# Threshold attention with a gated MLP on one core: attention products of 512 tokens in place of halves, and a new order on VectorE

## The chip, the core and the metric

The kernel runs on one core of a Trainium2 chip. Its engines work side by side, each through its own list of instructions in order: TensorE (PE; its weight loads are shown as PEld), VectorE (DVE), ScalarE (ACT), GpSimd (POOL) and SyncE (SP), which here issues DMAs. The metric is the device time of one execution in microseconds (us); lower is better. Times given as "the time" are medians over several executions; the profile comes from one execution, whose own time is given beside it.

## What is computed

Eight batches, eight heads, 576 tokens, head dimension 64. Scores that lie more than tau under their row's maximum are dropped, the rest goes through a softmax and multiplies v. The heads side by side are then the rows of a gated MLP ("MoE product" below) of 4608 tokens, 512 to 2048 to 512:

```
scores = scale * np.matmul(q, k.transpose(0, 1, 3, 2))
thresh = np.max(scores, axis=-1, keepdims=True) - tau
scores = np.where(scores >= thresh, scores, -1000000000.0)
attn = softmax(scores)
x = np.matmul(attn, v)            # heads side by side: 4608 x 512
h = x @ w_in
g = h * np.clip(h + 3.0, 0.0, 6.0) / 6.0
out = g @ w_out
```

## The kernel before, in words

**Units.** A pair is two heads of one batch, a quad is two pairs (16 quads in all). A quad is worked in nine slots: four of 128 query rows for its first pair, four for the second, and slot 8 for the last 64 rows of both. A slot holds both heads of a pair, so it is a tile of 128 rows x 2 x 576 keys. There are 16 x 9 = 144 slots, and one pass of the main loop, called a period n here, stands for each of them.

**Order.** Nothing is scheduled by a planner: the order of the program's statements is the order of each engine's list. From n = 22 on (N1 in the code) a period issues, by engine:

- DVE: the two maxima of slot n+1 (`sm_max`, line 302: it reads the scores from PSUM, writes them to SBUF and gives the row maximum), the reciprocal of slot n-1 (line 317), then what the list `waiting` holds (the scaling of a finished output tile into `osb`, line 423, or a query transpose), then the casts of the attention product (line 357, or 367 for the last rows), the rectifier of the MoE product where it is DVE's turn (line 391, odd periods), and the gate (line 404). In some odd periods a stream transpose of q or k follows (lines 241, 247).
- ACT: in even periods the rectifier (line 389); two exponentials of slot n (line 314) and two masks of slot n+1 (line 309).
- POOL: the bias of slot n+1 (line 305), the normalising of slot n-1 (line 322). SP then issues the DMA that transposes these probabilities into `pT`, the operand of the attention product, or into `pR` for slot 8; stores and loads follow.
- PE: a first MoE product (`mm1`, line 381 or 376), in odd periods an attention product if one is due (`av_main`, lines 346 and 349), in even periods two parts of the second MoE product (`mm2_part`, line 415), and at the end of odd periods the scores of slots n+3 and n+2 (line 287).

**PSUM.** The eight banks of 512 float columns are one tile `ps`. Scores of even slots lie in columns 128 to 703 and 1664 to 2239 (banks 0, 1, 3, 4). Scores of odd slots lie in 704 to 1279 and 2240 to 2815, and so take the first 256 columns of banks 2 and 5. Banks 2 and 5 are also those that `bank()` hands out in turn for attention products and transposes. First MoE products write bank 6 (`HB`; bank 7 in odd periods that follow an even one without second MoE parts), second ones bank 7 (`OB`). Hence three waits that the code implies:

- scores of slot n+3 (an even one, in an odd period n) may be written once the maxima of slot n+1 have read the same columns;
- scores of slot n+2 (odd) may be written once the attention product's cast has read banks 2 and 5, and once the maxima of slot n have;
- a first MoE product may be written once the gate of the period before has read bank 6.

**When a product is due.** The dictionary `products` says in which period which product is multiplied. Before, quads 0 and 1 take 512 tokens of a pair at once; from quad 2 on each pair is split into two products of 256 tokens, every second period. The function `multiply` issues them and, with the last ones of a batch, hands the first MoE products of that batch to the list `todo1`, of which one is taken in every period. An attention product is ten matmuls: four blocks of keys for each of two heads (line 346) and the last 64 keys (line 349); each head fills half of PE's columns, 64.

```
def av_main(pair, c0=0, w=512):
    ...
    pb = bank()[:, 0:w]
    av(pb, pair, pts[pair], slice(c0, c0 + w))
    return lambda: nc.vector.tensor_copy(out=xT[b][:, hp, c0:c0 + w], in_=pb)
```

**After the loop** the last products, the remaining MoE products and the stores follow.

Of the kernel before, what the change touches and what calls it, by code (L numbers as in the profile page):

```python
# [20 lines left out]
def kernel(  # L21
# [20 lines left out]
    N1 = 22  # L42
# [169 lines left out]
    def bank():  # L212
        nonlocal turn
        turn += 1
        return ps[:, (2, 5)[turn % 2], :]
# [96 lines left out]
    def sm_exp(sl, i):  # L312
        s = sl.s[:, i, :]
        nc.scalar.activation(out=s, in_=s, func=Act.Exp, accum_out=sl.rsum[:, i:i + 1])  # L314
# [26 lines left out]
    def av(pb, pair, pT, cols):  # L341
        b, hp = divmod(pair, NPAIR)
        vm, vr = vsb[b]
        for c in range(4):
            for a in range(2):
                nc.tensor.matmul(pb[a * 64:(a + 1) * 64, :], vm[:, 2 * hp + a, c * D:(c + 1) * D],  # L346
                                 pT[:, 5 * a + c, cols], start=(c == 0), stop=False)
        for a in range(2):
            nc.tensor.matmul(pb[a * 64:(a + 1) * 64, :], vr[:, a, hp, :], pT[:, 4, cols], start=False, stop=True)  # L349

    def av_main(pair, c0=0, w=512):
        b, hp = divmod(pair, NPAIR)
        if hp == c0 == 0:
            xT[b] = x_pool.tile([P, KI, 512], BF16, tag="xT", name="xT")
# [4 lines that stand above are left out]
    def av_rest(quad):  # L359
        b, g = divmod(quad, 2)  # L360
        pb = bank()
        for n in range(2):
            av(pb[:, n * 64:(n + 1) * 64], 2 * quad + n, ptr[quad], slice(n * 64, (n + 1) * 64))
        if b % 2 == 0 and g == 0:
            xR[b // 2] = x_pool.tile([P, KI, P], BF16, tag="xR", name="xR")
        o0 = 64 * (b % 2)
        return lambda: nc.vector.tensor_copy(out=xR[b // 2][:, 2 * g:2 * g + 2, o0:o0 + 64],
                                             in_=pb[:, 0:P].rearrange("p (a b) -> p a b", a=2))
# [17 lines left out]
    def mm1_relu(hps, on_act):  # L386
        r = r_pool.tile([P, 512], F32, tag="r", name="r")[:]
        if on_act:
            nc.scalar.activation(out=r, in_=hps, func=Act.Relu, bias=three[:])  # L389
        else:  # L390
            nc.vector.tensor_scalar(out=r, in0=hps, scalar1=3.0, scalar2=0.0, op0=Alu.add, op1=Alu.max)  # L391
        return r

    def mm1_gate(item, hps, r):
        b, ni, c0 = item
        if c0 is None:
            if ni % 8 == 0:
                odd[0] = go_pool.tile([P, 1024], BF16, name="go")
            out = odd[0][:, ni % 8 * P:ni % 8 * P + 512]
        else:  # L400
            c0 += (b % 2) * (S + 64)
            out = gbuf[:, ni:ni + 2, c0:c0 + 256]
            r, hps = (x.rearrange("p (n w) -> p n w", n=2) for x in (r, hps))
        nc.vector.scalar_tensor_tensor(out=out, in0=r, scalar=6.0, in1=hps, op0=Alu.min, op1=Alu.mult)  # L404
        if c0 is None and ni % 8 == 4:
            nc.sync.dma_start_transpose(out=gbuf[:, ni - 4:ni + 4, 512:512 + P], in_=odd[0][:])
# [87 lines left out]
    for quad in range(NQUAD):  # L494
        p0, p1 = 2 * quad, 2 * quad + 1
        if quad < NB:
            jobs = ((8, p0, 0, 512), (12, p1, 0, 512), (13, None, 0, 0))
        else:
            jobs = [(7 - quad % 2 + 2 * i, *of) for i, of in enumerate(
                ((p0, 0, 256), (p0, 256, 256), (p1, 0, 256), (p1, 256, 256), (None, 0, 0)))]  # L500
        for after, *of in jobs:
            products.setdefault(quad * NSLOT + after, []).append((quad, *of))

    def multiply(n):
        copies = []
        for of, pair, *columns in products.get(n, ()):
            copies.append(av_rest(of) if pair is None else av_main(pair, *columns))
            if of % 2 and pair is None:
                todo1.extend(moe_of(of // 2)[1])
            elif pair == 2 * of + 1 and of % 2 and columns[0] == 0:  # L510
                todo1.extend(moe_of(of // 2)[0])
        return copies

# [3 lines left out]
    waiting = []  # L517
    for n, sl in enumerate(queue):
        quad, slot = sl.quad, sl.slot
        b, g = divmod(quad, 2)  # L520
        now = n
        if slot in (0, 4):
            pts[2 * quad + slot // 4] = pt_pool.tile([P, 9, 512], BF16, tag="pT", name="pT")
        if slot == 8:
            ptr[quad] = ptr_pool.tile([P, 9, P], BF16, tag="pR", name="pR")
        for ahead in {0: (1, 2), 9: (3,), 16: (4,)}.get(n, (quad + 2,) if quad > 2 and slot == (2 if quad == 3 else 0) else ()):
            if ahead < NQUAD:
                load_quad(ahead)
        if slot == 0 and g == 1 and b + 1 < B:
            load_v(b + 1)  # L530
        for copy in last_keys:
            copy()
        last_keys = []
        if 0 < n <= N1:
            for i in range(2):
                sm_exp(prev, i)
        if n + 1 < len(queue):
            sm_max(queue[n + 1])
        even = n >= N1 and n % 2 == 0
        if n > N1:  # L540
            sm_recip(prev)
        for copy in waiting:
            copy()
        waiting = []

        if todo1:
            item, then = todo1.pop(0)
            h = mm1(item, OB if n > N1 and n % 2 and not pieces else HB)
            todo2.extend(then)
        else:  # L550
            item = None
        if n >= N1:
            for copy in multiply(n):
                copy()
        if item:
            mm1_gate(item, h, mm1_relu(h, on_act=even))
        copies = pe_transpose(queue[n - 2]) if n > 1 and queue[n - 2].on_chip else None
        if prev is not None and n < N1:
            sm_recip(prev)
        if copies:  # L560
            copies()
        pieces = 2 if n % 2 == 0 and todo2 else 0
        for _ in range(pieces):
            bb, mt, part = todo2.pop(0)
            mm2_part(bb, mt, part)
        if n <= N1:
            for i in range(2):
                sm_mask(sl, i)
        if n == N1:
            sm_recip(prev)  # L570
        if n >= N1:
            for i in range(2):
                sm_exp(sl, i)
            if n + 1 < len(queue):
                for i in range(2):
                    sm_mask(queue[n + 1], i)
        if n < N1:
            for copy in multiply(n):
                copy()
        if part == 3:  # L580
            waiting.append(lambda tile=(bb, mt): late.extend(mm2_out(*tile, on_act=False)))
            part = 0
        evict = []
        for job, of in turns.get(n, ()):
            if job == "k":
                (last_keys if even else evict).append(transpose_k(of))
            elif job == "q":
                if of // 2 not in qkT:
                    alloc_qk(of // 2)
                (waiting if even else evict).append(transpose_q(of))  # L590
            else:
                (last_keys if even else evict).append(transpose_rest(of, of_k=of > 0))
        for out_of_psum in evict:
            if out_of_psum:
                out_of_psum()
        if n == 0:
            warm_up(8)
        if n <= N1:
            scores(n + 2)
        elif n % 2:  # L600
            for m in (n + 3, n + 2):
                if m < len(queue):
                    scores(m)
        if n < 8:
            warm_up(6)
        if n > 0:
            sm_norm(prev)
        flush()
        if n == 0:
            start(loads, 2)  # L610
        elif n not in (4, 12, 15, 18, 21) and not 23 < n < 30 and (n < 37 or n % 2 == 0):
            start(loads, 1)
        if n < 4 or 15 < n < 20 or n > 33:
            start(vcasts, 1 if n < N1 or n % 2 else 0)
        else:
            start(casts, 2 if n in (5, 8, 11, 14) or 21 < n < 28 else 1)
        prev = sl
# [29 lines left out]
                count[1] += 1  # L647

    av_main(2 * last + 1, 0, 256)()
    for item in todo1:  # L650
        rest1(*item, on_act=False)
    sm_recip(prev)
# [45 lines left out]
```

## Time and profile before

| | |
|---|---|
| time, median of 5 executions | 522.43 us (521.38 to 523.4) |
| the profiled execution | 521.78 us, span of its instructions 520.0 us |
| granted TensorE clock | 1.000 |
| ACT and POOL, share of the span | 87% and 58% |
| scores on PE (line 287) | 174.0 us busy |
| first MoE products (381) and second (415) on PE | 130.8 and 123.4 us busy |
| attention products of 256 or 512 columns and of the last rows (346) | 39.1 us busy |
| maxima (302) on DVE | 205.1 us busy in 288 instructions |
| casts of 256 columns (357) on DVE | 23.5 us in 56, 420 ns each |
| casts of 512 columns (357) on DVE | 2.8 us in 4, 691 ns each |

How to read it: busy time is the union of an engine's instructions in the span. A matmul's own duration (273 ns at 256 columns) is longer than the time between two starts, since matmuls overlap; for what PE really needs, take the starts in the timeline. In timeline lines the columns are start, duration, engine, line, operation, output and inputs, shape, count, and in brackets the idle time before it with what ended it. Lines of one kind that follow each other are merged, and a few matmul records are missing from the trace (seven shown where eight are issued).

By stretches, the busy time of each engine is even from 104 us to 460 us (PE 57.5 of every 58.0 us, DVE 54.6, ACT 54.9). Before 80 us there are no MoE products; from 80 to 104 us there are hardly any second ones (PE 21.8 of 24 us, DVE 20.6, ACT 23.9); after 480 us the second MoE products of the end run on PE with little else.

### The profile page before, as it was taken

The numbers are of one execution on the slowest core, as the hardware profiler recorded it, in microseconds if no ns is written. First come the engines' busy times: TensorE is split into PE (matmuls) and PEld (weight loads), VectorE is DVE, ScalarE is ACT, GpSimd is POOL, SyncE is SP. The second block draws the span as 40 slices with busy tenths as digits, with TensorE's granted clock in tenths as the row PEclk, the third lists the DMA queues.
The fourth block names the chain that finished last, engine by engine and source line by source line (L and its number), as shares of the span: only waits on it lengthen the run. The fifth ranks groups of instructions, "written<-read, shape, count | busy, mean of one in ns | idle before, by whom it ended". The sixth has DMA issues, their size and how long they took to land.

```text
span 520.0 us, 12068 instructions
## 1 busy us (share of the span) xinstructions
PE 502.8 (97%) x4089; PEld 321.0 (62%) x4145; DVE 442.5 (85%) x1124; ACT 451.9 (87%) x980; POOL 299.3 (58%) x538
## 2 busy tenths in 40 slices
PE   8999899999999999999999999999999999999997
PEld 6765556666665666666655666666655666667463
DVE  3788888998999999999999999999999999877151
ACT  4999979999999999999999999999999999995060
POOL 1788869756676665657566756667566655551000
PEclk9999999999999999999999999999999999999999
DMA  5899899989999999999999999999999996564222
GB/s 131 129 171 169 143 147 146 195 140 177 167 169 165 158 179 165 179 172 185 171 157 166 178 177 158 174 167 173 172 166 165 168 170 113 112 117 65 83 61 61
DMA packets 314094, 78.77 MB, mean 151 GB/s; under 512 B 296624, under 2 KB 309168, under 8 KB 314032
## 3 DMA queue, kind: packets, MB, share of 16 engines
q1 hardware_dynamic: 294464, 67.90, 77.1%
q0 software_dynamic: 18368, 9.71, 15.5%
q8 instruction: 32, 0.52, 0.4%
q10 hardware_dynamic: 1200, 0.39, 0.3%
q14 instruction: 30, 0.25, 0.2%
HBM read 36.70 MB, written 9.44 MB: 89 GB/s over the span
## 4 chain that ended last, share of the span: by engine, by line
PE 77%; ACT 3%; DVE 2%; issue 2%; DMA 1%; POOL 0%; POOLq 0%; DVEq 0%
PE ps L287 24%; PE ps L415 23%; PE ps L381 19%; PE ps L346 6%; PE ps L376 2%; ACT s L309 1%; PE ps L349 1%; ACT s L314 1%; DMA pR<-pn 1%; ACT r L389 1%; DMA g<-go 1%; DVE s L302 1%; DVE g L404 1%; POOL pn L322 0%; PE ps L257 0%
## 5 line engine op out<-in xcount | busy, mean ns | idle before, releaser
L322 POOL TENSOR_SCALAR pn<-s,rinv 128x576 bf16<-128x576 f32 x288 | 210.6, 743 | 20.4 <-issue 4.4
L302 DVE TENSOR_SCALAR_CACHE_REDUCE s<-ps 128x576 f32<-128x576 f32 x288 | 205.1, 748 | 17.6 <-PE ps L287 9.0
L309 ACT ACTIVATE s<-s,bias 128x576 f32<-128x576 f32 x288 | 205.8, 763 | 6.0 <-POOL bias L305 5.7
L314 ACT ACTIVATE s<-s 128x576 f32<-128x576 f32 x288 | 192.5, 671 | 0.3
L287 PE MATMUL ps<-kT,qT 64*128 64x384 f32 (+7 forms) x1280 | 174.0, 419 | 4.7 <-DVE s L302 3.8
L287 PEld LDWEIGHTS ps<-kT,qT 64*128 64x128 f32 (+1 forms) x1280 | 103.6, 175 | 59.3 <-issue 15.8
L381 PE MATMUL ps<-xT,w_in_sb 128*128 128x256 bf16 x1024 | 130.8, 273 | 1.3 <-DVE g L404 0.7
L415 PE MATMUL ps<-w_out_sb,g 128*128 128x512 bf16 x524 | 123.4, 379 | 2.8 <-issue 0.2
L381 PEld LDWEIGHTS <-w_in_sb 128*128 128x128 bf16 x1024 | 95.5, 98 | 41.0 <-issue 22.1
L305 POOL TENSOR_SCALAR bias<-m 128x2 f32<-128x2 f32 x144 | 26.9, 187 | 152.9 <-DVE rinv L317 130.3
L404 DVE SCALAR_TENSOR_TENSOR g<-r,ps 128x512 bf16<-128x512 f32 x128 | 87.6, 687 | 9.6 <-ACT r L389 5.5
L415 PEld LDWEIGHTS <-g 128*128 128x128 bf16 x576 | 56.3, 98 | 56.6
L389 ACT ACTIVATE r<-ps,three 128x512 f32<-128x512 f32 x81 | 55.4, 687 | 29.0 <-PE ps L381 21.4
L314 ACT ACTIVATION_READ_ACCUMULATOR s<-s 128x1 f32 x288 | 54.5, 189 | 0.0
L391 DVE TENSOR_SCALAR r<-ps 128x512 f32<-128x512 f32 x63 | 42.9, 681 | 0.0
L346 PE MATMUL ps<-pT,vm 128*64 128x256 bf16 (+1 forms) x480 | 39.1, 285 | 0.0
L346 PEld LDWEIGHTS <-vm 128*64 128x64 bf16 x736 | 27.2, 110 | 17.0 <-issue 14.8
L357 DVE CAST xT<-ps 128x256 bf16<-128x256 f32 (+1 forms) x60 | 26.3, 438 | 12.8 <-PE ps L349 12.8
L423 DVE TENSOR_SCALAR osb<-ps 128x512 f32<-128x512 f32 x31 | 20.9, 673 | 13.3 <-PE ps L415 13.3
L302 DVE DVE_READ_ACCUMULATOR s<-ps 128x1 f32 x288 | 23.9, 83 | 0.0
L317 DVE RECIPROCAL rinv<-rsum 128x2 f32<-128x2 f32 x144 | 23.0, 160 | 0.6 <-ACT s L314 0.6
L143 POOL DMA_DIRECT2D vm<-in_v_dram x28 | 21.4, 766 | 0.7 <-issue 0.7
(57 smaller groups left out, 258.6 us busy)
## 6 DMA issues: line engine op xcount, KB each, us to landing
out_dram<-osb SPq DMA_DIRECT2D x31, 256.0 KB, 2.6
nq<-in_q_dram SPq DMA_DIRECT2D x96, 72.0 KB, 3.5
km<-in_k_dram SPq DMA_DIRECT2D x96, 64.0 KB, 3.3
vm<-in_v_dram POOLq DMA_DIRECT2D x24, 128.0 KB, 4.0
km<-in_k_dram SPq DMA_DIRECT2D x16, 128.0 KB, 3.6
w_in_sb<-in_moe_w_in_dram POOLq DMA_DIRECT2D x16, 128.0 KB, 3.6
w_out_sb<-in_moe_w_out_dram POOLq DMA_DIRECT2D x16, 128.0 KB, 4.3
pT<-pn SPq DMA_TRANSPOSE x117, 3.9
```

The source lines that it names most:

```text
L287: nc.tensor.matmul(ps_flat[rows, c0:c0 + w], qT_of(pair)[a * 64:(a + 1) * 64, q0:q0 + rows.stop - rows.start], kT_of(pair)[a * 64:(a + 1) ...
L302: nc.vector.tensor_scalar(out=sl.s[:, i, :], in0=ps_flat[:, c0:c0 + S], scalar1=1.0, scalar2=None, op0=Alu.mult, op1=Alu.max, accum_out=sl ...
L305: nc.gpsimd.tensor_scalar(out=sl.bias[:], in0=sl.m[:], scalar1=-scale, scalar2=tau, op0=Alu.mult, op1=Alu.add)
L309: nc.scalar.activation(out=s, in_=s, func=Act.Prelu, bias=sl.bias[:, i:i + 1], scale=scale, alpha=REJECT)
L314: nc.scalar.activation(out=s, in_=s, func=Act.Exp, accum_out=sl.rsum[:, i:i + 1])
L322: nc.gpsimd.tensor_scalar(out=pn[:, i, :], in0=sl.s[:, i, :], scalar1=sl.rinv[:, i:i + 1], scalar2=1.0, op0=Alu.mult, op1=Alu.mult)
L346: nc.tensor.matmul(pb[a * 64:(a + 1) * 64, :], vm[:, 2 * hp + a, c * D:(c + 1) * D], pT[:, 5 * a + c, cols], start=(c == 0), stop=False)
L381: nc.tensor.matmul(ps[:, hb, n * 256:(n + 1) * 256], w_in_sb[:, ki, (ni + n) * P:(ni + n + 1) * P], xT[b][:, ki, c0:c0 + 256], start=(ki = ...
L389: nc.scalar.activation(out=r, in_=hps, func=Act.Relu, bias=three[:])
L391: nc.vector.tensor_scalar(out=r, in0=hps, scalar1=3.0, scalar2=0.0, op0=Alu.add, op1=Alu.max)
L404: nc.vector.scalar_tensor_tensor(out=out, in0=r, scalar=6.0, in1=hps, op0=Alu.min, op1=Alu.mult)
L415: nc.tensor.matmul(o_ps[0], gbuf[:, ni, mt * P:(mt + 1) * P], w_out_sb[:, ni, :], start=(ni == 0), stop=(ni == NI - 1))
```

## The change

The periods in which attention products are due are set anew. From quad 2 on, in even quads both pairs are multiplied whole (512 tokens), in the slots where the second half used to be. In odd quads the first pair is whole and the second stays in halves. Three of four pairs are thus whole, and odd periods with a product and without one alternate for a part of the time. The condition that hands on the MoE products follows the new widths.

Within a period DVE's order changes: the rectifier of odd periods goes ahead of the cast of the attention product, and the copies in `waiting` go behind the gate. After the loop, `waiting` is flushed once.

```diff
         else:
-            jobs = [(7 - quad % 2 + 2 * i, *of) for i, of in enumerate(
-                ((p0, 0, 256), (p0, 256, 256), (p1, 0, 256), (p1, 256, 256), (None, 0, 0)))]
+            jobs = (((8, p0, 0, 512), (10, p1, 0, 256), (12, p1, 256, 256), (14, None, 0, 0)) if quad % 2 else
+                    ((9, p0, 0, 512), (13, p1, 0, 512), (15, None, 0, 0)))
         for after, *of in jobs:
             products.setdefault(quad * NSLOT + after, []).append((quad, *of))
...
-            elif pair == 2 * of + 1 and of % 2 and columns[0] == 0:
+            elif pair == 2 * of + 1 and of % 2 and columns == ([0, 256] if of > 1 else [0, 512]):
                 todo1.extend(moe_of(of // 2)[0])
...
-        for copy in waiting:
-            copy()
-        waiting = []
-
         if todo1:
             item, then = todo1.pop(0)
             h = mm1(item, OB if n > N1 and n % 2 and not pieces else HB)
             todo2.extend(then)
         else:
             item = None
-        if n >= N1:
-            for copy in multiply(n):
-                copy()
+        copies = multiply(n) if n >= N1 else []
         if item:
-            mm1_gate(item, h, mm1_relu(h, on_act=even))
+            r = mm1_relu(h, on_act=even)
+        for copy in copies:
+            copy()
+        if item:
+            mm1_gate(item, h, r)
+        for copy in waiting:
+            copy()
+        waiting = []
...
     av_main(2 * last + 1, 0, 256)()
+    for copy in waiting:
+        copy()
     for item in todo1:
```

`None` in a job stands for the product of the last 64 rows of both pairs of a quad (slot 8), called the rest product below.

## The prediction

> **What bounds the kernel now.** I read the page first: busy shares, then the chain that ended last. Its lines, with "..." where others are left out:
>
> ```profile
> PE 502.8 (97%) x4089; PEld 321.0 (62%) x4145; DVE 442.5 (85%) x1124; ACT 451.9 (87%) x980; POOL 299.3 (58%) x538
> ...
> PE 77%; ACT 3%; DVE 2%; issue 2%; DMA 1%; POOL 0%; POOLq 0%; DVEq 0%
> ```
>
> TensorE (PE) is hardly ever idle and carries the chain, so the time is what PE has to do plus the few places where it waits. But a 97% average doesn't say how near the other engines are. So I took the timeline of PE for one pair of periods in the steady part: the odd period with the product, then the even one.
>
> ```profile
> 259.25 1.03 PE L381 MATMUL ps<-xT,w_in_sb 128*128 128x256 bf16 x8
> 260.21 0.63 PE L346 MATMUL ps<-pT,vm 128*64 128x256 bf16 x8
> 260.67 0.28 PE L349 MATMUL ps<-pT,vr 128*64 128x256 bf16 x2
> 260.88 2.21 PE L287 MATMUL ps<-kT,qT 64*128 64x384 f32 x16
> 263.02 1.05 PE L381 MATMUL ps<-xT,w_in_sb 128*128 128x256 bf16 x8
> 264.12 1.67 PE L415 MATMUL ps<-w_out_sb,g 128*128 128x512 bf16 x7
> 265.63 0.60 PE L381 MATMUL ps<-xT,w_in_sb 128*128 128x256 bf16 x4
> ```
>
> Call the first start T. From start to start: first MoE product 0.96 us (0.97 in most pairs), half an attention product 0.67, two slots of scores 2.14, then first and second MoE product 2.61; the pair takes 6.38. VectorE (DVE) over the same time:
>
> ```profile
> 258.50 0.69 DVE L404 SCALAR_TENSOR_TENSOR g<-r,ps 128x512 bf16<-128x512 f32 x1 [0.26 <-ACT r L389]
> 259.11 0.75 DVE L302 TENSOR_SCALAR_CACHE_REDUCE s<-ps 128x576 f32<-128x576 f32 x1
> ...
> 259.78 0.75 DVE L302 TENSOR_SCALAR_CACHE_REDUCE s<-ps 128x576 f32<-128x576 f32 x1
> ...
> 260.46 0.16 DVE L317 RECIPROCAL rinv<-rsum 128x2 f32<-128x2 f32 x1
> 260.99 0.42 DVE L357 CAST xT<-ps 128x256 bf16<-128x256 f32 x1 [0.36 <-PE ps L349]
> 261.33 0.68 DVE L391 TENSOR_SCALAR r<-ps 128x512 f32<-128x512 f32 x1
> 262.04 0.69 DVE L404 SCALAR_TENSOR_TENSOR g<-r,ps 128x512 bf16<-128x512 f32 x1
> ```
>
> What the reader is to see: the even gate ends at 259.19 and PE's next first MoE product, which needs that bank, starts at 259.25. The two maxima of the odd period stand behind this gate in DVE's order. The second ends at 260.53, that is at T+1.28. PE comes to the scores at T+1.63. These scores (slot n+3, an even one) go into the very columns that those maxima (slot n+1, even too) have just read. So today the half product hides the maxima, with 0.3 us to spare. The third view is a place where it doesn't hide them, early in the run, where even periods have no second MoE product:
>
> ```profile
> 97.33 0.75 DVE L302 TENSOR_SCALAR_CACHE_REDUCE s<-ps 128x576 f32<-128x576 f32 x1
> ...
> 98.00 0.75 DVE L302 TENSOR_SCALAR_CACHE_REDUCE s<-ps 128x576 f32<-128x576 f32 x1
> ```
>
> ```profile
> 98.14 2.18 PE L287 MATMUL ps<-kT,qT 64*128 64x384 f32 x12 [0.98 <-DVE s L302]
> ```
>
> PE waits 0.98 us: its first score starts 0.06 after the first maximum's end (98.08), its weight loads go on at 98.82, 0.07 after the second's end (98.75), and the next MoE product starts at 100.95, 2.13 after that. So two slots of scores take their full 2.14 counted from 0.07 after the second maximum; the head start of one matmul is worth nothing.
>
> **What the Trainium skill says.** TensorE: Matmul & The Clock Gate, Back-to-back issue gap, prices a warm matmul at N/2.4 + 2.5 ns (109 ns at 256 columns, 216 at 512); TensorEngine Tiling (Array Packing), Key Properties, says that tiles run in parallel and that a change of tiling mode drains the engine. Ten matmuls, two column tiles at a time, are then 0.55 us at 256 and 1.08 at 512; the trace has 0.67 and 1.20, so a fixed 0.12 per product is left, which agrees with a drain but doesn't prove one. Perfetto Trace Analysis, Optimizing Scalar/DVE Operations, gives DVE a fixed cost per instruction and says that larger operations improve throughput; the trace agrees (two casts of 0.42 against one of 0.69). The same section adds that where an engine causes bubbles elsewhere, work broken up may finish sooner, which is this case seen from behind.
>
> **The change part by part.**
>
> *Merging.* 21 pairs of half products become whole ones. The whole product's price is in the trace, from the four at the start (all 1.20):
>
> ```profile
> 33.88 1.05 PE L346 MATMUL ps<-pT,vm 128*64 128x512 bf16 x8
> 34.76 0.38 PE L349 MATMUL ps<-pT,vr 128*64 128x512 bf16 x2
> 35.08 1.24 PE L287 MATMUL ps<-kT,qT 64*128 64x384 f32 x8
> ```
>
> Each merge saves PE 2 x 0.67 - 1.20 = 0.14 us, and DVE 2 x 0.42 - 0.69 = 0.15. On PE at most 21 x 0.14 = 2.9. Of these, 18 (odd periods 35 to 139) lie where PE is bound: -2.5. The other three (27, 31, 143) are taken below.
>
> *Where the product goes.* In a cycle of 18 periods (nine pairs) every odd one holds a half today, but for one with only the rest product. After: 1 and 3 half, 5 rest, 7 none, 9 whole, 11 none, 13 whole, 15 rest, 17 whole. Whole ones come one or two periods later than the first half did, at the second half's place, so what reads xT, the pT buffers and the transposes into them see no later date.
>
> *Odd periods with none.* PE is ready for scores at T+0.97. DVE can't be earlier: the even gate comes a fixed time after the even MoE product (ACT's rectifier between; 263.02 to 264.82, then 0.69, ends 2.49 after it), PE comes round 2.61 after it, and the maxima follow the gate. In the pair at 265.63 the second maximum starts at 266.10 and ends at 266.85: scores from T+1.29, wait 0.32. In the pair at 259.25 the gate is later and the same sum gives 1.35, wait 0.38. One of each kind in a cycle: 0.70. There are 12 such periods beyond n=40 (43, 47, 61, 65, 79, 83, 97, 101, 115, 119, 133, 137): 6 x 0.70 = +4.2. The wait stands ahead of everything PE has queued: the scores, both MoE products and all after. PE's pair is then 6.38 - 0.67 + 0.35 = 6.06. ACT needs 5.94 for its own pair (relu 0.62, four exponentials and four masks in four groups of 1.33), so it would have taken 0.2 of this itself had the maxima been sooner.
>
> *Odd periods with a whole product.* PE: product ends T+2.17, second slot of scores starts T+3.24. DVE, from maxima at T-0.2: rectifier 1.23 to 1.94, cast from 2.28 (product's end plus the 0.11 of 260.88 to 260.99) to 2.97, gate to 3.58, output copy to 4.1, stream transpose to 4.8, even maxima to 6.1, gate 6.2 to 6.9. The scores that write over the product's columns need the cast: 2.97 against 3.24, 0.2 spare. PE's next turn is at 6.92 and the gate with its 0.06 at 6.95 where copy and transpose fall together: nothing to 0.05. I take +0.1 in all. If the cover of 0.2 were gone, the cost is what exceeds it, 18 times.
>
> *Rectifier first.* In half periods it fills DVE's idle 0.36 ahead of the cast, so gates end about 0.3 sooner; PE's next need there is already met (gate ends 262.73, needed 263.02), so 0. Without it, whole periods would have gate and rectifier behind a 0.69 cast.
>
> *Copies moved behind the gate.* The output copy goes from T+1.4 to about T+3.5. It frees a bank that PE takes again in the next even period (T+4.4 at the earliest), and SP issues the store 2 us later, behind the same transposes as before; loads behind it have half a batch of time. Query transposes of quad 3 move likewise, long before their scores. 0. The flush added after the loop finds nothing left to copy: 0.
>
> *The early and the last merge.* At n=25 and 29 PE waits 1.01 and 0.98 for maxima with a half ahead of it; taking the half out makes the wait longer, not the period shorter. At 27 the whole product ends at 92.05, before the scores can start (92.43): 0. At 31 PE is bound and pays 1.20 for 0.67: +0.5. At 141 the half goes and the rectifier comes first, so the gate that PE waits for (0.66 at 463.34) ends up to 0.9 sooner; ACT, only 0.45 early there, allows 0.5; 143 pays 0.53 more: about 0.
>
> *Sum:* -2.5 + 4.2 + 0.1 + 0.5 = +2.3 us. The profiled execution is 520.0 of span plus 1.8 around it, 521.78, and would become 524.1; it lies 0.65 below the median of 522.43, so I forecast a median of 524.7. Bounds: waits of 0.28 to 0.40 (3.4 to 4.8), merges 0.13 to 0.15 each, the early merge 0 to 0.5, the end -0.4 to +0.2, DVE or ACT late in whole periods 0 to 1.0. That makes +0.3 to +4.2, own range 522.8 to 526.6.
>
> **The rivals.**
> *The merging pays in full* (faster). If the maxima don't bind, PE keeps its 2.9 us: 519.5. For it: PE is 97% busy, and the fixed 0.12 is seen in all halves. Against: the maxima end at T+1.28 in the trace, with no sooner place for them. It decides if the wait per empty period is under 2.5/12 = 0.2.
> *Half the wait* (no change). Part of the scores slips under the maxima and a wait of about 0.2 remains: 12 x 0.2 - 2.5 + 0.1 = 0, 522.4. Against it is the place at 98.14.
> *The casts come late* (slower still). DVE drifts by 0.5 and whole periods wait for the cast as well: 18 x 0.3 = 5.4 more, 530. For it: in the pair at 265.63, with output copy and transpose, DVE has no gap. Against: the order resets at every even gate.
>
> **How the numbers follow.** A measurement of this kernel can't tell less than 0.2% (1.04 us) from no change. Forecast 0.70, full saving 0.13, half the wait 0.12, late casts 0.05. The forecast's own lower end gives a twentieth to "same" and the half-wait case spreads to both sides: slower 0.74, same 0.12, faster 0.14. The range reaches from 520.6, which takes in part of the faster case and all of "same", to 526.6.
>
> **What would show it.** In the profile after: 42 fewer casts of 256 and 21 more of 512; whole products at about 1.20; in the empty odd periods, PE's scores waiting for DVE's L302 with about 0.3 between the MoE product and the scores, and a pair of about 6.05; whole pairs about 6.92; idle time before L287 up by some 4 us while PE's busy time falls. Wrong if those gaps are absent (then faster), or if PE's gaps stand in the whole periods instead (casts, gates).

## The result, and the profile after

The changed kernel takes 525.02 us (median of 31 executions, 523.87 to 527.33) against 522.49 us (52 executions) measured beside it: the ratio is 1.006, 95% interval 1.0051 to 1.007. It is slower by 2.5 us. Its times fall into two clusters, taken up under "The clock" below; the profiled execution took 524.7 us with a span of 523.0 and belongs to the lower one.

The scores' row on TensorE from the page of the kernel before, then the busy line and the same row from the page of the kernel after:

```profile
L287 PE MATMUL ps<-kT,qT 64*128 64x384 f32 (+7 forms) x1280 | 174.0, 419 | 4.7 <-DVE s L302 3.8
```

```profile
PE 506.1 (97%) x3888; PEld 318.5 (61%) x3935; DVE 437.9 (84%) x1103; ACT 452.0 (86%) x980; POOL 299.3 (57%) x538
...
L287 PE MATMUL ps<-kT,qT 64*128 64x384 f32 (+7 forms) x1280 | 178.1, 419 | 5.7 <-DVE s L302 4.6
```

There are 210 matmuls less to do, DVE has 4.6 us less, and yet TensorE is busy for 3.3 us more. The scores did not change at all, and their busy time grew from 174.0 to 178.1 us. So the page already says where to look, and it says it as busy time, not as idle time.

The timeline shows why. This is TensorE of the kernel after in an empty odd period, one without an attention product (n=43), and from the end of the whole product of the next odd one (n=45); columns as before.

```profile
144.73 1.03 PE L381 MATMUL ps<-xT,w_in_sb 128*128 128x256 bf16 x8
145.69 2.60 PE L287 MATMUL ps<-kT,qT 64*128 64x384 f32 x16
148.22 1.05 PE L381 MATMUL ps<-xT,w_in_sb 128*128 128x256 bf16 x8
149.10 1.89 PE L415 MATMUL ps<-w_out_sb,g 128*128 128x512 bf16 x8
150.83 1.04 PE L381 MATMUL ps<-xT,w_in_sb 128*128 128x256 bf16 x8
```

```profile
152.69 0.38 PE L349 MATMUL ps<-pT,vr 128*64 128x512 bf16 x2
153.00 2.21 PE L287 MATMUL ps<-kT,qT 64*128 64x384 f32 x16
155.14 1.04 PE L376 MATMUL ps<-w_in_sb,xR 128*128 128x512 bf16 x3
```

VectorE of the same kernel in the empty period:

```profile
144.59 0.75 DVE L302 TENSOR_SCALAR_CACHE_REDUCE s<-ps 128x576 f32<-128x576 f32 x1
...
145.27 0.75 DVE L302 TENSOR_SCALAR_CACHE_REDUCE s<-ps 128x576 f32<-128x576 f32 x1
...
146.02 0.67 DVE L391 TENSOR_SCALAR r<-ps 128x512 f32<-128x512 f32 x1
```

With T = 144.73, the second maximum ends at 146.02 = T+1.29. The scores begin at T+0.96 with the one matmul that may run, and hold until then: from their start to the next MoE product it is 2.53 us in the empty period and 2.14 in the whole one (153.00 to 155.14). The difference, 0.39, is the wait. It doesn't count as idle, because the profile shows a first score matmul as 0.59 us long in both periods. In the empty one the second starts 0.39 after the first (145.69 to 146.08), in the whole one at once, so the first one's shown length covers the wait. The 12 empty periods beyond n=40 show 0.39 or 0.38 (nine) and 0.32 (three): 4.4 us.

To see the whole path, take the start T of single odd periods in the two profiles, counted from the first attention product (33.88 us before, 34.88 after: this 1.00 lies in the first loads, ahead of anything that was changed, and the experiments' profiles have 33.9 to 35.0 there).

| us | before | after | difference |
|---|---|---|---|
| first product to n=31 | 69.79 | 70.39 | +0.60 |
| n=31 to 41 | 32.64 | 33.04 | +0.40 |
| n=41 to 131, five cycles of 18 periods | 291.21 | 293.20 | +1.99 (0.40 a cycle) |
| n=131 to 141 | 31.96 | 32.39 | +0.43 |
| n=141 to 143 | 6.46 | 5.83 | -0.63 |
| n=143 to the end | 50.25 | 49.43 | -0.82 |
| in all | 482.31 | 484.28 | +1.97 |

### The profile page after: what moved, and what is told of

The parts are those of the page before. It is cut to its first block, busy times and chain, and to the rows that moved or that the text cites. A ratio compares the mean times of both kernels' runs of the same rounds, so it can differ in the third digit from the quotient of the medians.

```text
span 523.0 us, 11683 instructions
## 1 busy us (share of the span) xinstructions
PE 506.1 (97%) x3888; PEld 318.5 (61%) x3935; DVE 437.9 (84%) x1103; ACT 452.0 (86%) x980; POOL 299.3 (57%) x538
## 4 chain that ended last, share of the span: by engine, by line
PE 79%; ACT 4%; DVE 1%; issue 1%; DMA 1%; POOL 0%; POOLq 0%; DVEq 0%
PE ps L287 25%; PE ps L415 23%; PE ps L381 21%; PE ps L346 6%; PE ps L376 2%; ACT s L309 2%; ACT s L314 2%; PE ps L349 1%; ACT r L389 1%; DMA g<-go 1%; DVE g L404 1%; DVE s L302 0%; POOL pn L322 0%; PE ps L257 0%; ACT kT L222 0%
## 5 line engine op out<-in xcount | busy, mean ns | idle before, releaser
L287 PE MATMUL ps<-kT,qT 64*128 64x384 f32 (+7 forms) x1280 | 178.1, 419 | 5.7 <-DVE s L302 4.6
L287 PEld LDWEIGHTS ps<-kT,qT 64*128 64x128 f32 (+1 forms) x1280 | 109.2, 175 | 62.8 <-DVE s L302 12.7
L415 PE MATMUL ps<-w_out_sb,g 128*128 128x512 bf16 x536 | 129.6, 379 | 2.2 <-issue 0.2
L346 PE MATMUL ps<-pT,vm 128*64 128x512 bf16 (+1 forms) x312 | 35.1, 347 | 0.0
L357 DVE CAST xT<-ps 128x512 bf16<-128x512 f32 (+1 forms) x39 | 23.1, 592 | 9.7 <-PE ps L349 9.7
L346 PEld LDWEIGHTS <-vm 128*64 128x64 bf16 x568 | 20.2, 110 | 16.9 <-issue 10.9
```

What stands on the lines that cost most here:

```text
L287: nc.tensor.matmul(ps_flat[rows, c0:c0 + w], qT_of(pair)[a * 64:(a + 1) * 64, q0:q0 + rows.stop - rows.start], kT_of(pair)[a * 64:(a + 1) ...
L415: nc.tensor.matmul(o_ps[0], gbuf[:, ni, mt * P:(mt + 1) * P], w_out_sb[:, ni, :], start=(ni == 0), stop=(ni == NI - 1))
```

## The experiments

Edits are against the changed kernel where nothing else is said. Ratios are to the kernel before, run beside each.

**1. The new order alone.** Attention products as before, VectorE's order as after.

```diff
-            jobs = (((8, p0, 0, 512), (10, p1, 0, 256), (12, p1, 256, 256), (14, None, 0, 0)) if quad % 2 else
-                    ((9, p0, 0, 512), (13, p1, 0, 512), (15, None, 0, 0)))
+            jobs = [(7 - quad % 2 + 2 * i, *of) for i, of in enumerate(
+                ((p0, 0, 256), (p0, 256, 256), (p1, 0, 256), (p1, 256, 256), (None, 0, 0)))]
...
-            elif pair == 2 * of + 1 and of % 2 and columns == ([0, 256] if of > 1 else [0, 512]):
+            elif pair == 2 * of + 1 and of % 2 and columns[0] == 0:
```

> Halves as in the kernel before, with the new order on VectorE alone. Theory (the cost sits in odd periods without a product): no period is empty, so the pair stays at 6.38 us; the query copy that now stands behind the gate costs what the trace after shows near 86 us, about 0.6, at most; 522.5 to 523.2. Rival (the new order itself costs): the whole loss or most of it, 524.5 or more.

Measured: 521.34 us, ratio 0.9984 (0.9975 to 0.9992). The order costs nothing in all; it gains 0.8 us, which neither theory had said. A cycle takes 58.21 us against 58.24 before, so the gain isn't in the steady part. In its profile it loses 0.68 up to n=31 and gains 0.63 from n=141 to 143 and 1.06 after that.

**2. The whole products alone**, with VectorE's order as in the kernel before.

```diff
+        for copy in waiting:
+            copy()
+        waiting = []
...
-        copies = multiply(n) if n >= N1 else []
-        if item:
-            r = mm1_relu(h, on_act=even)
-        for copy in copies:
-            copy()
-        if item:
-            mm1_gate(item, h, r)
-        for copy in waiting:
-            copy()
-        waiting = []
+        if n >= N1:
+            for copy in multiply(n):
+                copy()
+        if item:
+            mm1_gate(item, h, mm1_relu(h, on_act=even))
```

> Whole products in the new places, VectorE's order as before. Theory: empty periods still wait for the maxima, 12 x 0.35 = 4.2 us, so about 524.5 to 525; in whole periods rectifier and gate come behind a cast that waits to T+2.28, the gate ends near T+4.3 where TensorE needs it at T+4.31, so 0 to 0.1 in each of 18, up to 527. Rival (order is the cost): back to 519.5 to 522.5.

Measured: 526.61 us, ratio 1.0086 (1.0064 to 1.0107), at the upper part of what the theory allowed and against the rival. Three of its six executions are in the upper cluster; the other three have 526.1. The empty periods wait as before (scores 2.53), and the whole ones now lose too: in its timeline TensorE goes from 152.82 to 157.16 (4.34, against 4.31) and from there to 159.85 (2.69, against 2.60). A cycle takes 58.92 us, 0.28 more than with the new order. So whole products cost 0.68 a cycle, and the new order gives 0.28 of it back. Rectifier first and copies last changed together here, so the runs don't say which of the two does it.

**3. The scores of an empty period the other way round.**

```diff
-            for m in (n + 3, n + 2):
+            for m in (n + 3, n + 2) if n in products else (n + 2, n + 3):
```

> The changed kernel, but in odd periods without a product the scores of slot n+2 go before those of n+3, so that nothing waits for the maxima of n+1. Theory: the wait of 0.35 is gone from TensorE, but ScalarE needs 5.94 us for a pair that TensorE would do in 5.71, and its rectifier, late by 0.2, holds the gate and the next MoE product: a pair of about 5.9 in place of 6.05 to 6.1, 12 x 0.17 = 2.0 us gained, about 523.0. If ScalarE is not in the way: 12 x 0.35 = 4.2 gained, 520.8. Rival (maxima are not the cause): 525 as it is.

Measured: 525.62 us, ratio 1.0067 (1.0044 to 1.009), and the cycle 58.64 us, the same as in the changed kernel. On TensorE of this kernel:

```profile
145.83 1.03 PE L381 MATMUL ps<-xT,w_in_sb 128*128 128x256 bf16 x8
146.80 2.60 PE L287 MATMUL ps<-kT,qT 64*128 64x320 f32 x16
149.33 0.50 PE L381 MATMUL ps<-xT,w_in_sb 128*128 128x256 bf16 x3
```

Slot n+2 now goes first (a form with 320 columns leads), and still the group takes 2.53. By its result alone this run would speak for the rival. But look at the group from inside, in stretches of 0.15 us (start and end, length, busy time and number of the scores' matmuls, the same of their weight loads, granted clock, DMA share, GB/s), and at what VectorE does meanwhile:

```profile
146.85:147.00 0.15, 0.15 (x1) 0.15 (x2) 1.00 0.68 150
147.00:147.15 0.15, 0.15 (x1) 0.09 (x1) 1.00 1.27 288
147.15:147.30 0.15, 0.15 (x3) 0.11 (x3) 1.00 1.28 292
```

```profile
146.37 0.75 DVE L302 TENSOR_SCALAR_CACHE_REDUCE s<-ps 128x576 f32<-128x576 f32 x1
```

Up to 147.15 only the matmul that started at 146.80 is there. The second maximum of slot n+1 ends at 147.12. The next weight load of the scores stands in the trace with a wait for a semaphore that VectorE raises, and it starts at 147.19. So the swap had not removed the wait it was made to remove. The first 320 columns of slot n+2 lie at 704 and 2240, in banks 1 and 4; the maxima of slot n+1 read 128 to 703 and 1664 to 2239, and so parts of the same two banks. No column is shared, but the bank is, and in this program the waits go by the bank. The list of three waits under "PSUM" above lacks this one.

**4. More work in the empty periods.**

```diff
         elif n % 2:
+            if n > 40 and n not in products:
+                for i in range(2):
+                    nc.tensor.transpose(ps[:, 2 + 3 * i, 256:384], identf[:], identf[:])
             for m in (n + 3, n + 2):
```

> The changed kernel with two more 128-column f32 transposes of the identity (about 0.28 us) on TensorE ahead of the scores in each of the 12 empty odd periods beyond n=40; their result is not used. Theory: they fall into the wait for the maxima and cost nothing, 525.0 +- 0.3. Rival (TensorE waits for nothing there, its own work sets the pair): 12 x 0.28 = 3.4 more, 528.4.

Measured: 526.26 us in 6 executions, ratio 1.0072 (1.0048 to 1.0097), an interval that holds the changed kernel's 1.006 and not the 1.011 of the rival (528.4). Three of the six are in the upper cluster; the other three have a median of 525.17. The trace is sharper. TensorE of this kernel, in a part at full clock (line 604 is the filler):

```profile
146.58 1.03 PE L381 MATMUL ps<-xT,w_in_sb 128*128 128x256 bf16 x8
147.45 0.38 PE L604 MATMUL ps<-identf 128*128 128x128 f32 x2
147.76 2.38 PE L287 MATMUL ps<-kT,qT 64*128 64x384 f32 x16
150.07 0.39 PE L381 MATMUL ps<-xT,w_in_sb 128*128 128x256 bf16 x2
```

From first MoE product to first MoE product it is 3.49 us, as in the changed kernel without the filler (144.73 to 148.22), and the cycle is again 58.64. 0.3 us of work fits into the wait and costs nothing.

**5. The piece that waits for nobody goes first.** Of slot n+2's scores the 256 columns in banks 2 and 5 share no bank with the maxima.

```diff
-    def scores(n):
+    def scores(n, parts=(0, 1)):
...
-        for k0, w in ((0, w0), (w0, S - w0)):
+        for k0, w in [((0, w0), (w0, S - w0))[p] for p in parts]:
...
-            for m in (n + 3, n + 2):
+            steps = ((n + 3, (0, 1)), (n + 2, (0, 1)))
+            if n > 40 and n not in products:
+                steps = ((n + 2, (1,)), (n + 3, (0, 1)), (n + 2, (0,)))
+            for m, parts in steps:
                 if m < len(queue):
-                    scores(m)
+                    scores(m, parts)
```

> The changed kernel; in its empty odd periods beyond n=40 the 256 columns of slot n+2 in banks 2 and 5 go first, then slot n+3, then the 320 columns of slot n+2 in banks 1 and 4, which the maxima of slot n+1 still read when the swap put them first. The piece takes about 0.46 us (256 of 1152 columns in 2.14), so TensorE comes to slot n+3 at T+1.43, after the maxima. Theory (the wait is for the banks that the maxima read, and ScalarE is next): pair of 5.9 in place of 6.05 to 6.1, 12 x 0.17 = 2.0 us less than the changed kernel, ratio to before about 1.002. If ScalarE isn't next: 4.2 less, ratio 0.998. If the maxima are not what is waited for: no gain, 1.006.

Measured: 522.07 us, ratio 1.001 (0.9997 to 1.0022): most of the loss is gone. TensorE of this kernel at n=43 and 44:

```profile
144.87 1.03 PE L381 MATMUL ps<-xT,w_in_sb 128*128 128x256 bf16 x8
145.84 2.21 PE L287 MATMUL ps<-kT,qT 64*128 64x256 f32 x16
147.98 1.05 PE L381 MATMUL ps<-xT,w_in_sb 128*128 128x256 bf16 x8
148.86 1.89 PE L415 MATMUL ps<-w_out_sb,g 128*128 128x512 bf16 x8
150.77 1.03 PE L381 MATMUL ps<-xT,w_in_sb 128*128 128x256 bf16 x8
```

The scores take 2.14 again. The pair takes 5.90 and not 5.72: the even period is 2.79 long in place of 2.61. ScalarE of this kernel says by what:

```profile
147.99 1.43 ACT L309 ACTIVATE s<-s,bias 128x576 f32<-128x576 f32 x2
149.32 0.67 ACT L389 ACTIVATE r<-ps,three 128x512 f32<-128x512 f32 x1
```

The MoE product ends at 149.03, the rectifier follows without a gap behind the masks at 149.32, and the gate behind it at 150.03. This is the turn at ScalarE that the theory named, but only in one of the two empty periods of a cycle; the other (n=47, period 11 of the cycle) gets nearly all of its 0.35. A cycle gains 0.51 on the changed kernel, where 0.34 was expected.

**6. The rectifier between the masks**, on top of 5: in an empty period the second mask waits in a list, and is issued behind the rectifier of the next period.

```diff
+        while held:
+            sm_mask(held.pop(), 1)
...
-                for i in range(2):
-                    sm_mask(queue[n + 1], i)
+                sm_mask(queue[n + 1], 0)
+                if n > 40 and n % 2 and n not in products:
+                    held.append(queue[n + 1])
+                else:
+                    sm_mask(queue[n + 1], 1)
```

> As the one with the piece first, and ScalarE's second mask of an empty period is moved behind the rectifier of the even period after it, so that the rectifier can start when its MoE product is there. Theory: if ScalarE is what holds the pair once the maxima don't, most of the other 2 us comes too: about 4.4 less than the changed kernel, ratio to before about 0.998; pairs of 5.72 to 5.8. If ScalarE was not in the way, the same as the one with the piece first.

Measured: 524.07 us, ratio 1.0028 (1.0016 to 1.004), a miss. A cycle takes 58.16 us, against 58.13 with 5. At n=44 the even period is 2.61 as hoped, but the one at n=50 grows from 2.60 to 2.77, where the rectifier starts behind the masks again (171.61; its MoE product ended at 171.34): ScalarE has the same work and is late a little further on. In the next cycle nothing is gained: n=62 stays at 2.85, as with 5. The higher median comes from something else, below.

**7. Quad 2 in halves again, and early copies in their old place**, on top of 6.

```diff
         if n > N1:
             sm_recip(prev)
+        if n < 31:
+            for copy in waiting:
+                copy()
+            waiting = []
...
-        if quad < NB:
+        if quad == 2:
+            jobs = [(7 + 2 * i, *of) for i, of in enumerate(
+                ((p0, 0, 256), (p0, 256, 256), (p1, 0, 256), (p1, 256, 256), (None, 0, 0)))]
+        elif quad < NB:
```

> As the one with the rectifier between the masks, quad 2 back in halves, and the copies in the waiting list ahead of the products as before up to n=30. Theory: the 0.6 that the moved query copy costs near 86 us and the 0.4 to 0.5 of the early merge are gone: 1.0 to 1.1 less than that kernel, ratio to before about 0.996.

Measured: 521.0 us, ratio 0.9979 (0.9969 to 0.9989): 3.1 less than 6, three times what was expected of it. Most of that is the clock, taken up behind experiment 8; against the lower cluster of 6 (521.74) it is 0.7, less than the 1.0 to 1.1 expected.

**8. The order alone, early copies in their old place.** Experiment 1 with the first part of that edit.

> Halves as in the kernel before, with the new order on VectorE, but the copies in the waiting list stay ahead of the products up to n=30. Theory: the order gains at the end (about 1.7 in the trace of the order alone) and loses 0.7 near 86 us through the moved query copy; without the loss 0.7 less than the order alone, ratio to before about 0.997.

Measured: 521.02 us, ratio 0.9978 (0.9971 to 0.9985). From the first product to n=31 it takes 69.88 us, against 70.47 in experiment 1: the moved query copy had cost 0.6. The end is another matter: from n=141 on this kernel gains 0.76 on the kernel before, where experiment 1, the same program there, gained 1.69. In its profile TensorE waits for the last transposed probabilities, as it does before (the line is shown further down), and in that of experiment 1 it doesn't:

```profile
478.43 0.32 PE L346 MATMUL ps<-pR,vm 128*64 128x64 bf16 x8 [0.81 <-DMA pR<-pn]
```

**The clock.** The times of experiment 6 fall into two clusters, 521.65 to 521.94 and 523.73 to 524.67, and the mean granted TensorE clock parts them: 0.997 to 1.0 in the six of the lower one, 0.992 or 0.993 in the 12 of the upper. The changed kernel does the same: of the 32 executions that list a clock, 18 have 0.997 to 1.0 (median 524.75) and 14 have 0.993 (median 526.93). The kernel before has none under 0.998 in the 91 executions that list a clock, experiments 1, 7 and 8 none in 56. TensorE's wait at n=25 differs between the two sorts of kernel; first before, then after:

```profile
85.72 2.88 PE L287 MATMUL ps<-kT,qT 64*128 64x384 f32 x16 [1.01 <-DVE s L302]
```

```profile
86.72 2.45 PE L287 MATMUL ps<-kT,qT 64*128 64x384 f32 x12 [1.68 <-DVE s L302]
```

The stretches of two profiles (start and end, length, TensorE busy, matmuls, granted clock, DMA share, GB/s) show the place. First the kernel after, in an execution at full clock:

```profile
85.10:86.80 1.70, 0.08 (x1) 1.00 1.34 194
86.80:88.50 1.70, 1.70 (x11) 1.00 1.84 187
88.50:90.20 1.70, 1.48 (x10) 1.00 0.72 131
90.20:91.90 1.70, 1.06 (x10) 1.00 1.30 202
```

Then experiment 6, whose program is the same up to there:

```profile
85.10:86.80 1.70, 0.03 (x2) 1.00 1.38 213
86.80:88.50 1.70, 1.70 (x10) 1.00 1.24 215
88.50:90.20 1.70, 1.70 (x9) 0.56 1.28 224
90.20:91.90 1.70, 1.70 (x11) 0.50 1.24 196
```

At n=25 TensorE waits 1.68 us for the maxima, since the half product that stood there is gone. In the execution of experiment 6 (1.67) the clock falls to half some 2 us after that wait has ended, stays there for about 3.4 us, and does so again after the wait at n=29 (0.57 and 0.50 from 102.1 to 105.5). In the execution of the kernel after nothing falls, with the same wait at n=25. What decides between executions isn't known. From the first product to n=31 that execution of experiment 6 takes 73.18 us in place of 70.4.

**9. More work for TensorE in periods 25 and 29.**

```diff
         elif n % 2:
+            if n in (25, 29):
+                warm_up(5)
             for m in (n + 3, n + 2):
```

> The changed kernel with five more 128-column f32 transposes of the identity (about 0.7 us, result not used) on TensorE ahead of the scores in periods 25 and 29, where TensorE waits 1.7 and 1.3 us since the half products have gone. Theory (those two waits let TensorE's clock fall to half for some 3.4 us each in nearly half of the executions, 14 of 31 for the changed kernel with a mean clock under 0.998): no execution with a mean clock under 0.998, times in one cluster near 524.7 to 525. Rival (the low clock has another cause): clusters near 524.7 and 526.9 as before.

Measured: 524.2 us, ratio 1.0043 (1.0031 to 1.0056), five executions within 523.92 and 524.67, all with a clock of 0.999 or 1.0. The ratio is that of the changed kernel's lower cluster (524.75 to 522.49). The transposes write bank 6 and so first wait for a gate themselves:

```profile
85.51 0.77 PE L185 MATMUL ps<-identf 128*128 128x128 f32 x5 [1.00 <-DVE g L404]
```

So TensorE isn't busy throughout; its longest stretch of waiting is cut from 1.68 to 1.00, what it is with the half product. With 14 of 32 falling before, five in a row by chance would be 0.06 (18/32 to the fifth), so this run alone is not proof. With experiment 7, where the halves do the same (none in 13, where 6 had 12 of 18), and with all runs taken together the cause is well supported. The six kernels without the half at n=25 and without this filler (the changed one and experiments 2 to 6) have a clock of 0.995 or less in 37 of 82 executions. The other six (before, 1, 7, 8, 9, 10) have none under 0.998 in 157.

**10. The piece first, quad 2 in halves, early copies in their old place;** ScalarE as it was.

> The kernel with the piece first, with quad 2 back in halves and the copies in the waiting list ahead of the products up to n=30, ScalarE's order untouched. Theory: at full clock 521.9 less 0.6 (query copy) less 0.4 to 0.5 (early merge) = 520.8 to 520.9, no execution with the low clock, ratio to before about 0.9975: about what the order alone gives with the early copies left in place. If the rectifier between the masks was worth something, slower than the kernel that had it (0.9979).

Measured: 520.38 us, ratio 0.9966 (0.9952 to 0.9979), five executions at 0.999 or 1.0. It beats the kernel before by 1.7 us and, by the two ratios, the changed one by more than 4. It isn't slower than 7, so no gain from the rectifier between the masks is seen. Against the order alone with early copies in place (experiment 8, 0.9978, run at another time) the intervals overlap, so it isn't shown that whole products are worth anything even with the wait taken out. In this profile and in that of 7 a further wait appears at n=91, for transposed probabilities (0.54 us here, 0.66 in 7), which 5 doesn't have:

```profile
299.36 0.63 PE L346 MATMUL ps<-pT,vm 128*64 128x256 bf16 x8 [0.54 <-DMA pT<-pn]
```

## Why the prediction was right, and where it wasn't

*The place and the wait* were right: the empty odd periods wait for the maxima of slot n+1, 0.39 and 0.32 to 0.38 where 0.38 and 0.32 were worked out, 4.4 us where 4.2 were. Experiments 4 and 5 show it by filling the wait and by removing it. The signs named for the rest came too: 14 casts of 256 columns and 25 of 512, whole products at 1.20, whole pairs at 6.91 to 6.92, and nothing of the 0.1 allowed for late casts and gates. That ScalarE is next was right in kind, but it holds only one of the two empty periods of a cycle.

*What the merging saves* was sized a little too high. Whole products cost TensorE 1.20 as taken, and the empty period drops 0.67 of work. But the third half in a cycle stood behind a rest product, and there the step from both (4.25 us for the period) to the rest alone (3.71) is 0.54. The third merge of a cycle so saves 0.01 and not 0.14. A cycle loses 0.40, not 0.28: 0.7 us in six, of which 0.2 are the slightly longer waits. The prediction's 0.55 and 1.08 us for ten matmuls, from which it took a fixed part of 0.12, are estimates from the price that the Trainium skill (TensorE: Matmul & The Clock Gate, Back-to-back issue gap) gives for a matmul by itself. This trace has 216 ns at 512 columns (eight in 1.73 us, line 415), as that price has, but 121 at 256 (eight in 0.97, line 381) where the price is 109. So how much of a product is fixed isn't settled; what is measured is that two halves cost 0.14 more than a whole.

*The copies moved behind the gate at nothing* was a step that failed. At n=24 a query transpose by TensorE leaves its copy (line 239) in the list, and at n=25 the scores of slot 27 wait for the bank that it reads. TensorE of the kernel after:

```profile
86.72 2.45 PE L287 MATMUL ps<-kT,qT 64*128 64x384 f32 x12 [1.68 <-DVE s L302]
89.39 0.70 PE L287 MATMUL ps<-kT,qT 64*128 64x256 f32 x4 [0.22 <-DVE qT L239]
90.02 1.05 PE L381 MATMUL ps<-xT,w_in_sb 128*128 128x256 bf16 x8
91.71 0.55 PE L232 MATMUL ps<-identf,km 128*128 128x128 f32 x3 [0.64 <-DVE s L302]
```

The prediction had asked when the query would be needed, and not who needs the bank. It cost 0.6 us with halves, shown by experiment 8 against 1, where the same wait for line 239 is 0.42. In the changed kernel, where the first wait at n=25 is longer too, the loss up to n=31 is 0.60 as well.

*The early merge* (0.5 at n=31, with 35's saving 0.4) came out at 0.40 from n=31 to 41. That a longer wait at n=25 and 29 would cost nothing holds in executions at full clock; in the others it costs about 2.2 us (526.93 against 524.75).

*The end at nothing* was wrong the other way. From n=141 on the changed kernel gains 1.45 us in its profile, and the order alone 1.69. The gate of n=141, which TensorE waits for, comes sooner, as worked out: 0.63 up to n=143 in both. More follows behind the loop: before, TensorE waits there for the last transposed probabilities,

```profile
478.48 0.32 PE L346 MATMUL ps<-pR,vm 128*64 128x64 bf16 x8 [0.78 <-DMA pR<-pn]
```

and in the kernel after it doesn't wait at that line. The prediction had not looked for that gain at all. But experiment 8, with the new order, has the same wait again (0.81), so whether this 0.78 comes from the change or varies between executions is open.

*Rectifier first at nothing* was right for half periods (58.21 against 58.24 a cycle). In whole ones the new order saves 0.28 a cycle, which the prediction said of the rectifier without a figure.

That the sum came out is in part luck: the early loss (0.6) and the missed saving (0.7) stand against the missed gain at the end (1.45). The low clock was not foreseen either. At full clock the change costs 524.75 - 522.49 = 2.3 us, the forecast figure; the low clock moves the median by 0.3 more.

*A sign that was named wrongly:* TensorE's busy time was to fall and its idle time before the scores to rise by 4 us. Its busy time rose by 3.3, and that idle time by 1.0. The wait is inside the group of scores, behind their first matmul, which the prediction had itself seen to go ahead alone at 98.14.

*The rivals:* full saving needed a wait under 0.2; half the wait needed part of the scores to slip under the maxima. Neither was seen. Late casts are what experiment 2 has in part (0.03 in the odd period, 0.09 in the even one), but not the changed kernel.

## What to carry to other kernels

Work on the bound engine can be the cover of a wait: before it is taken out of a period, ask what the engine will reach sooner, and whether that is ready. Merging two pieces saves their overhead once, but moves work from one period into another, and here the time that the empty periods lost in waiting was not made up in the whole ones. A copy that is moved later holds its bank longer, whoever wants its result: here 0.6 us. And where a wait seems to hang on columns, ask which bank they lie in.

## What the runs showed of the hardware

- In the profile of experiment 6 a wait of TensorE of 1.67 us, with 0.03 us busy in a stretch of 1.70, was followed by a granted clock of 0.50 to 0.56 over about 3.4 us. The six kernels whose programs leave this wait (1.67 or 1.68 in five of their six profiles) had a mean clock of 0.995 or less in 37 of 82 executions; the six with 1.00 or 1.01 there had it in none of 157. In the profile of the changed kernel waits of 1.68 and 1.30 (n=29) had no such effect. Such an execution of the changed kernel is 2.2 us longer in the median, and its mean clock over the whole span shows it only in the third decimal.
- A short wait inside a group of matmuls can be shown as busy: a first score matmul is shown as 0.59 us long, and the second started 0.39 after it. The scores' groups grew from 2.14 to 2.53 us, their busy time by 4.1 us in all, their idle time by 1.0.
- Ten matmuls of 64-column tiles take 0.67 us for 256 columns and 1.20 for 512, so two halves cost 0.14 more than a whole. Where such a product follows another one a part of this is saved: 0.54 in place of 0.67 for the half behind a rest product.
